# Weight decode in a top-k attention and ELU kernel: the sign word made on GpSimd and joined by VectorE

## The chip, the cores and the metric

The kernel runs on one core of a Trainium2 chip. The metric is device time in microseconds (us) of one execution; lower is better. Before the change three runs took 1666.97, 1667.17 and 1669.18 us, median 1667.17 us. The engines are named as in the profile: PE is TensorE (PEld its weight loads), DVE is VectorE, ACT is ScalarE, POOL is GpSimd, SP is SyncE, which here only issues DMAs.

## The reference

Attention over 8 batches, 8 heads, 576 positions and 64 dimensions per head, in which each query row keeps only its 32 largest scores, followed by a two-layer network with an ELU between its layers.

```python
def _attn_ref(q, k, v):
    B, H, S, D = q.shape            # 8, 8, 576, 64
    top_k = 32
    scores = (1.0 / np.sqrt(D)) * np.matmul(q, k.transpose(0, 1, 3, 2))
    kth = np.partition(scores, -top_k, axis=-1)[..., -top_k:-top_k + 1]
    scores = np.where(scores >= kth, scores, -1000000000.0)
    scores = scores - np.max(scores, axis=-1, keepdims=True)
    attn = np.exp(scores)
    attn = attn / (np.sum(attn, axis=-1, keepdims=True) + 1e-09)
    return np.matmul(attn, v).astype(np.float32)

def _moe_ref(x, w_in, w_out):       # x: 4608 x 512, w_in: 512 x 2048, w_out: 2048 x 512
    h = x @ w_in
    g = np.where(h > 0.0, h, np.exp(np.minimum(h, 0.0)) - 1.0)
    return (g @ w_out).astype(np.float32)
```

The two weight matrices arrive as 64-bit floats. The kernel gets each as pairs of 32-bit words (low word, high word) and has to make 32-bit floats of them on the chip before the network can use them. That decode is the part that the change touches.

## The kernel before, in words

**Attention.** The work is a list of steps; a step is one tile of 128 query rows for one pair of heads. For each step PE makes the scores (L299), ACT moves them to SBUF (L307), and DVE finds the 32 largest of each row: four MAX8 instructions with three MATCH_REPLACE8 between them, for each of the two heads (`select_row` in the first eight steps, lines 318 to 328; `select` afterwards, lines 341 to 353). Then `mask` makes two tiny operands on POOL (`neg` L366, `gap` L368) and runs Prelu and Exp on ACT (L369, L370); `normalise` runs five tiny POOL operations and two of 128x576 (L380 to L387); `turn` transposes on PE (L406) and copies on ACT (L407); `attend` multiplies by V on PE (L432) and ACT copies the result (L459).

**Network.** As soon as the attention output of a block of tokens is complete, its network pieces are queued: `hidden` (PE L504; ACT L514, L517, L519; DVE L476) and `project` (PE L529; ACT L538). `feed` lets pieces go by a plan of due steps, and only when enough weights are decoded (`decoded[0]`).

**Decode.** The two matrices are cut into 32 pieces of 128x512 numbers. `load_weight(i)` brings the raw piece, 512 KB of word pairs, into one of seven buffers named `raw` (L153, on SP's queue). In the raw tile the low and the high words alternate, so each of them is read with a step of two words. Before the change a piece then goes through:

- ACT L174: the low word, as an integer, to a float (Copy with scale and bias, so that the bits hold the low mantissa), in place
- ACT L175: the sign of the high word (Sign), written as one byte of fp8 into every eighth byte of the tile
- ACT L178: the magnitude of the high word (Abs with a scale), in place
- POOL L179: the magnitude held between a largest and a smallest value (min, max), in place
- DVE L186: the high word shifted left by three, in place
- POOL L187: the integer sum of the high and the low word, written to the final weight tile `w_in` or `w_out`

**Order.** `decode_piece(i)` issues the load of piece i+3, `convert_first(i)` (the first four operations) and `convert_last(i - 3)` (the last two). There are 35 such calls in a list. `hook()`, called by the selection after its later rounds, takes one from the list: four per step in the first eight steps (two for each head), then three in step 8. When the list is empty the raw buffers are closed and the network's larger tiles take their place. For the first two transposes and from step 8 on (`n == tight`) each engine's order is the program's; in between, in the first eight steps, a scheduler orders each engine's queue by readiness and program order at compile time. On the chip every engine then works its queue strictly in order.

Of the kernel before, what the change touches and what calls it, by code (L numbers as in the profile page):

```python
# [8 lines left out]
AF = mybir.ActivationFunctionType  # L9
ALU = mybir.AluOpType  # L10
FP32 = mybir.dt.float32
U32 = mybir.dt.uint32
I32 = mybir.dt.int32
FP8 = mybir.dt.float8e4
PSUM = bass.MemoryType.PSUM

TOP_K = 32
# [64 lines left out]
def kernel(  # L82
# [9 lines left out]
    nc = tc.nc  # L92
# [9 lines left out]
    NF = dff // P  # L102
# [3 lines left out]
    scale = 1.0 / float(D) ** 0.5  # L106
# [33 lines left out]
    raw = {}  # L140

    def weight(i):
        per = dff // WN
        if i < NC * per:
            f, c = divmod(i, NC)
            src = moe_w_in[c * P : (c + 1) * P, 2 * f * WN : 2 * (f + 1) * WN]
            return src, w_in[:, c, f * WN : (f + 1) * WN]
        f = i - NC * per
        return moe_w_out[f * P : (f + 1) * P, :], w_out[:, f, :]

    def load_weight(i):
        t = rawpool.tile([P, 2 * WN], U32, tag="raw", name="raw")
        nc.sync.dma_start(t[:], weight(i)[0])  # L153
        raw[i] = t

    def parts(t):
        words = t[:].rearrange("p (n w) -> p n w", w=2)
        signs = t[:].bitcast(FP8).rearrange("p (n w) -> p n w", w=8)
        return words[:, :, 0], words[:, :, 1], signs[:, :, 3]

    def convert_first(i):

        lo, hi, sign = parts(raw[i])
        ef, mf = hi.bitcast(FP32), lo.bitcast(FP32)
        nc.scalar.activation(mf, lo, AF.Copy, scale=2.0**-35, bias=2.0**17)  # L174
        nc.scalar.activation(  # L175
            sign, ef, AF.Sign, scale=2.0**64, bias=1.0, saturate=False
        )
        nc.scalar.activation(ef, ef, AF.Abs, scale=2.0**-62)  # L178
        nc.gpsimd.tensor_scalar(  # L179
            ef, ef, (2.0 - 2.0**-3 - 2.0**-23) * 2.0**-46, 2.0**-77, ALU.min, ALU.max  # L180
        )

    def convert_last(i):
        t, dst = raw.pop(i), weight(i)[1]
        lo, hi, sign = parts(t)
        nc.vector.tensor_single_scalar(hi, hi, 3, ALU.logical_shift_left)  # L186
        nc.gpsimd.tensor_tensor(  # L187
            dst.bitcast(I32), hi.bitcast(I32), lo.bitcast(I32), ALU.add
        )

    decode = []
    decoded = [0]
# [10 lines left out]
            late["x"] = ctx.enter_context(tc.tile_pool(name="xt", bufs=2))  # L203

    def decode_piece(i):
        if i < 2 * NF:
            if i + 3 < 2 * NF:
                load_weight(i + 3)
            convert_first(i)
        if i > 2:  # L210
            convert_last(i - 3)
            decoded[0] = i - 2

    loaded, kqT, vT = {}, {}, {}

# [200 lines left out]
    def attend(g):  # L416
# [28 lines left out]
        while tiles:  # L445
            blk, lo, parts = tiles[0].block, tiles[0].cols.start, 0
            while tiles and tiles[0].block is blk:
                parts += 1
                hi = tiles.pop(0).cols.stop
            finish(blk, parts, g.hp, slice(lo, hi), ps[:, c0 : c0 + hi - lo])  # L450
            c0 += hi - lo
# [106 lines left out]
    for b in range(B):  # L558
# [12 lines left out]
        for qt in range(J + 1):  # L571
# [8 lines left out]
            t = Tile(b, qt, rows, blk, slice(c0, c0 + n))  # L580
# [6 lines left out]
        for qts in order:  # L587
# [3 lines left out]
            for qt in qts:  # L591
                n = len(steps)
# [54 lines left out]
    for hp in range(1, NHP):  # L647
        load_v(0, hp)
    decode += [lambda i=i: decode_piece(i) for i in range(2 * NF + 3)]
    at(0, start_qk, 0, 2)  # L650
    at(1, start_qk, 0, 3)
# [93 lines left out]
```

## Time and profile before

| | value |
|---|---|
| median of three runs | 1667.17 us (1666.97 to 1669.18) |
| the profiled execution's own time | 1667.02 us |
| its span, first to last instruction | 1665.2 us |
| PE busy | 1592.8 us, 96% of the span |
| DVE busy | 1495.8 us, 90% |
| ACT busy | 1165.1 us, 70% |
| POOL busy | 630.5 us, 38% |
| mean granted TensorE clock | 0.977 |

Busy time is summed over the whole span, which hides that the stages differ. The kernel has three: an opening of some 150 us in which the 32 weight pieces are decoded beside the first nine steps; a long middle; and a tail of about 100 us without selection, in which PE finishes the last network blocks. The page cuts the span into 40 slices of 41.6 us; a digit is the busy share of a slice in tenths. A time stamp such as "at 57.39" counts in us from the span's start.

### The profile page before, as it was taken

The numbers are of one execution on the slowest core, as the hardware profiler recorded it, in microseconds if no ns is written. First come the engines' busy times: TensorE is split into PE (matmuls) and PEld (weight loads), VectorE is DVE, ScalarE is ACT, GpSimd is POOL, SyncE is SP. The second block draws the span as 40 slices with busy tenths as digits, with TensorE's granted clock in tenths as the row PEclk, the third lists the DMA queues.
The fourth block names the chain that finished last, engine by engine and source line by source line (L and its number), as shares of the span: only waits on it lengthen the run. The fifth ranks groups of instructions, "written<-read, shape, count | busy, mean of one in ns | idle before, by whom it ended". The sixth has DMA issues, their size and how long they took to land.

```text
span 1665.2 us, 25986 instructions
## 1 busy us (share of the span) xinstructions
PE 1592.8 (96%) x8528; PEld 1031.5 (62%) x8528; DVE 1495.8 (90%) x3044; ACT 1165.1 (70%) x2377; POOL 630.5 (38%) x1719
## 2 busy tenths in 40 slices
PE   5589999999999999999999999999999999999999
PEld 3366677657574767656566676755557575755565
DVE  5887999999999999999999999999999999998500
ACT  6998777668686777678667685868758585857521
POOL 3775444333334334333334333333333343332200
PEclk9578999999999999999999999999999999999999
DMA  7540120001100110001100111001200100000000
GB/s 211 171 144 7 23 50 29 7 15 44 48 1 8 43 42 22 1 28 37 42 14 1 50 29 35 1 14 43 50 13 1 28 15 29 7 7 7 7 13 13
DMA packets 101126, 56.21 MB, mean 34 GB/s; under 512 B 84096, under 2 KB 92288, under 8 KB 100992
## 3 DMA queue, kind: packets, MB, share of 16 engines
q1 hardware_dynamic: 99792, 54.26, 11.7%
q8 instruction: 68, 1.11, 0.3%
q14 instruction: 66, 0.54, 0.1%
q10 hardware_dynamic: 1200, 0.30, 0.1%
HBM read 45.09 MB, written 9.44 MB: 33 GB/s over the span
## 4 chain that ended last, share of the span: by engine, by line
PE 65%; DVE 21%; ACT 9%; POOL 3%; issue 2%; SPq 0%; DMA 0%; ACTq 0%; POOLq 0%; DVEq 0%
PE ops L529 24%; PE hps L504 20%; DVE wk L346 9%; DVE m L353 8%; PE avps L432 7%; PE scps L299 6%; PE eps L406 5%; DVE m L341 3%; ACT sc L370 2%; ACT sc L369 1%; DVE gT L476 1%; ACT raw L175 1%; PE qkps L269 1%; ACT et L407 1%; POOL w_in L187 1%
## 5 line engine op out<-in xcount | busy, mean ns | idle before, releaser
L353 DVE MAX8 m<-wk 128x8 f32<-128x576 f32 x816 | 577.0, 750 | 0.0
L504 PE MATMUL hps<-xT,w_in 128*128 128x256 f32 (+2 forms) x2432 | 548.1, 374 | 12.5 <-ACT xT L459 12.3
L529 PE MATMUL ops<-w_out,gT 128*128 128x512 f32 x1152 | 522.8, 598 | 0.0
L504 PEld LDWEIGHTS hps<-xT,w_in 128*128 128x128 f32 x2432 | 406.5, 193 | 109.2 <-issue 23.8
L346 DVE MATCH_REPLACE8 wk<-m,wk 128x576 f32<-128x576 f32 x544 | 400.8, 746 | 0.0
L529 PEld LDWEIGHTS ops<-w_out,gT 128*128 128x128 f32 x1152 | 208.7, 190 | 233.0 <-issue 219.5
L380 POOL TENSOR_SCALAR dene<-den 128x2 f32<-128x2 f32 x144 | 35.9, 249 | 771.2 <-ACT sc L370 770.6
L369 ACT ACTIVATE sc<-sc,neg 128x576 f32<-128x576 f32 x288 | 226.8, 788 | 89.2 <-POOL neg L366 89.0
L370 ACT ACTIVATE sc<-sc,gap 128x576 f32<-128x576 f32 x288 | 224.1, 778 | 25.7 <-ACT sc L369 0.7
L387 POOL TENSOR_SCALAR sc<-sc,rec 128x576 f32<-128x576 f32 x288 | 221.0, 778 | 14.9
L307 ACT ACTIVATE sc<-scps 128x576 f32<-128x576 f32 x288 | 174.0, 659 | 73.3 <-PE scps L299 73.3
L299 PE MATMUL scps<-kqT 64*128 64x288 f32 (+1 forms) x1280 | 201.8, 440 | 21.2 <-ACT kqT L275 7.9
L407 ACT COPY et<-eps 128x512 f32<-128x512 f32 x288 | 166.8, 579 | 55.2 <-PE eps L406 55.0
L346 DVE MATCH_REPLACE8 wk<-m,sc 128x576 f32<-128x576 f32 x272 | 200.4, 746 | 0.0
L432 PE MATMUL avps<-et,vT 128*64 128x256 f32 (+2 forms) x2080 | 193.3, 326 | 4.8 <-ACT et L407 4.6
L406 PEld LDWEIGHTS eps<-ident,sc 128*128 128x128 f32 x1152 | 143.6, 144 | 83.8 <-issue 46.2
L476 DVE SCALAR_TENSOR_TENSOR gT<-n,gT 128x512 f32<-128x512 f32 (+1 forms) x132 | 100.2, 759 | 102.0 <-ACT n L519 101.9
L341 DVE MAX8 m<-sc 128x8 f32<-128x576 f32 x272 | 191.8, 748 | 0.0
L406 PE MATMUL eps<-ident,sc 128*128 128x128 f32 x1152 | 175.7, 278 | 15.4 <-POOL sc L387 13.0
L432 PEld LDWEIGHTS avps<-et,vT 128*64 128x64 f32 x2080 | 122.6, 141 | 79.1 <-issue 22.8
L299 PEld LDWEIGHTS scps<-kqT 64*128 64x128 f32 (+1 forms) x1280 | 108.1, 181 | 91.9 <-issue 44.2
L514 ACT ACTIVATE n<-hps 128x512 f32<-128x512 f32 (+1 forms) x156 | 88.0, 564 | 71.4 <-PE hps L504 67.5
(47 smaller groups left out, 1170.2 us busy)
## 6 DMA issues: line engine op xcount, KB each, us to landing
kin<-in_k_dram SPq DMA_DIRECT2D x64, 128.0 KB, 2.8
raw<-in_moe_w_in_dram SPq DMA_DIRECT2D x16, 512.0 KB, 5.4
vT<-in_v_dram SPq DMA_DIRECT2D x64, 128.0 KB, 2.3
raw<-in_moe_w_out_dram SPq DMA_DIRECT2D x16, 512.0 KB, 3.9
out_dram<-osb SPq DMA_DIRECT2D x32, 256.0 KB, 2.3
qin<-in_q_dram SPq DMA_DIRECT2D x62, 128.0 KB, 2.8
kin<-in_k_dram SPq DMA_DIRECT2D x32, 32.0 KB, 2.4
vT<-in_v_dram SPq DMA_DIRECT2D x64, 16.0 KB, 2.2
```

Of the source, the lines that this page charges most:

```text
L299: nc.tensor.matmul(wide[i][rows, half, 0:HS], kq[part, q0 : q0 + u.t.ql], kq[part, k0 : k0 + HS], start=True, stop=True,)
L341: nc.vector.max(found[i], cur[i])
L346: nc.vector.match_replace(wk[i], found[i], cur[i], TAKEN)
L353: nc.vector.max(found[i], cur[i])
L369: nc.scalar.activation(sc, sc, AF.Prelu, bias=neg[:], alpha=STEEP)
L370: nc.scalar.activation(sc, sc, AF.Exp, bias=gap[:], accum_out=u.den[:, i : i + 1])
L387: nc.gpsimd.tensor_scalar(u.sc[:, i, :], u.sc[:, i, :], rec[:, i : i + 1], 1.0, ALU.mult, ALU.mult)
L406: nc.tensor.transpose(ps[:, c * P : (c + 1) * P], sc[:, c0 : c0 + P], ident[:])
L407: nc.scalar.copy(g.et[:, chunks, u.at, :], ps[:, 0 : n * P].rearrange("p (c q) -> p c q", c=n),)
L432: nc.tensor.matmul(ps[i * D : (i + 1) * D, cols], vt[:, 2 * J + i if c == J else i * J + c, :], w, start=(c == 0), stop=(c == J),)
L504: nc.tensor.matmul(blk.h[:, f % bank, :], w_in[:, i, f * P : (f + 1) * P], blk.xT[:, i, 0:n_tok], start=(i == 0), stop=(i == NC - 1),)
L529: nc.tensor.matmul(blk.o[:], blk.gT[f // NG][:, f % NG, s * P : (s + 1) * P], w_out[:, f, :], start=(f == 0), stop=(f == NF - 1),)
```

## The change

The sign is no longer made on ACT as a byte of fp8. The magnitude is written by ACT straight into the final weight tile. POOL holds it between its bounds there, and in a second, new operation multiplies the raw high word, taken as a float, by zero, which leaves a zero with the sign of the number. DVE's shift becomes a two-input operation that shifts the magnitude in the weight tile left by three and joins the sign word by exclusive or. POOL adds the low word in place. The four parts of a piece are now spread over four consecutive calls, instead of the first and the fourth.

```diff
     def convert_first(i):
-        lo, hi, sign = parts(raw[i])
-        ef, mf = hi.bitcast(FP32), lo.bitcast(FP32)
-        nc.scalar.activation(mf, lo, AF.Copy, scale=2.0**-35, bias=2.0**17)
-        nc.scalar.activation(
-            sign, ef, AF.Sign, scale=2.0**64, bias=1.0, saturate=False
-        )
-        nc.scalar.activation(ef, ef, AF.Abs, scale=2.0**-62)
-        nc.gpsimd.tensor_scalar(
-            ef, ef, (2.0 - 2.0**-3 - 2.0**-23) * 2.0**-46, 2.0**-77, ALU.min, ALU.max
+        lo, hi = parts(raw[i])
+        nc.scalar.activation(weight(i)[1], hi.bitcast(FP32), AF.Abs, scale=2.0**-66)
+        nc.scalar.activation(lo.bitcast(FP32), lo, AF.Copy, scale=2.0**-35, bias=2.0**17)
+
+    def convert_second(i):
+        w = weight(i)[1]
+        nc.gpsimd.tensor_scalar(
+            w, w, (2.0 - 2.0**-3 - 2.0**-23) * 2.0**-50, 2.0**-81, ALU.min, ALU.max
         )
+        ef = parts(raw[i])[1].bitcast(FP32)
+        nc.gpsimd.tensor_scalar(ef, ef, 0.0, 1.0, ALU.mult, ALU.mult)
+
+    def convert_third(i):
+        w = weight(i)[1].bitcast(U32)
+        nc.vector.scalar_tensor_tensor(
+            out=w, in0=w, scalar=3, in1=parts(raw[i])[1],
+            op0=ALU.logical_shift_left, op1=ALU.bitwise_xor,
+        )

     def convert_last(i):
-        t, dst = raw.pop(i), weight(i)[1]
-        lo, hi, sign = parts(t)
-        nc.vector.tensor_single_scalar(hi, hi, 3, ALU.logical_shift_left)
-        nc.gpsimd.tensor_tensor(
-            dst.bitcast(I32), hi.bitcast(I32), lo.bitcast(I32), ALU.add
-        )
+        w, t = weight(i)[1].bitcast(I32), raw.pop(i)
+        nc.gpsimd.tensor_tensor(w, w, parts(t)[0].bitcast(I32), ALU.add)
...
     def decode_piece(i):
-        if i < 2 * NF:
-            if i + 3 < 2 * NF:
-                load_weight(i + 3)
-            convert_first(i)
-        if i > 2:
-            convert_last(i - 3)
-            decoded[0] = i - 2
+        stages = (convert_first, convert_second, convert_third, convert_last)
+        if i + 3 < 2 * NF:
+            load_weight(i + 3)
+        for ago, stage in enumerate(stages):
+            if 0 <= i - ago < 2 * NF:
+                stage(i - ago)
+        decoded[0] = max(0, i - 2)
```

More of the change, by code (lines that the diff above doesn't have):

```diff
@@ L13 @@
 I32 = mybir.dt.int32
-FP8 = mybir.dt.float8e4
 PSUM = bass.MemoryType.PSUM
@@ L157, in parts @@
         words = t[:].rearrange("p (n w) -> p n w", w=2)
-        signs = t[:].bitcast(FP8).rearrange("p (n w) -> p n w", w=8)
-        return words[:, :, 0], words[:, :, 1], signs[:, :, 3]
+        return words[:, :, 0], words[:, :, 1]
     def convert_first(i):
-        lo, hi, sign = parts(raw[i])
-        ef, mf = hi.bitcast(FP32), lo.bitcast(FP32)
-        nc.scalar.activation(mf, lo, AF.Copy, scale=2.0**-35, bias=2.0**17)
-        nc.scalar.activation(
-            sign, ef, AF.Sign, scale=2.0**64, bias=1.0, saturate=False
-        )
-        nc.scalar.activation(ef, ef, AF.Abs, scale=2.0**-62)
-        nc.gpsimd.tensor_scalar(
-            ef, ef, (2.0 - 2.0**-3 - 2.0**-23) * 2.0**-46, 2.0**-77, ALU.min, ALU.max
+        lo, hi = parts(raw[i])
[5 more added lines that the diff above has]
+            w, w, (2.0 - 2.0**-3 - 2.0**-23) * 2.0**-50, 2.0**-81, ALU.min, ALU.max
+        )
+        ef = parts(raw[i])[1].bitcast(FP32)
[5 more added lines that the diff above has]
+            op0=ALU.logical_shift_left, op1=ALU.bitwise_xor,
         )
     def convert_last(i):
-        t, dst = raw.pop(i), weight(i)[1]
-        lo, hi, sign = parts(t)
-        nc.vector.tensor_single_scalar(hi, hi, 3, ALU.logical_shift_left)
-        nc.gpsimd.tensor_tensor(
-            dst.bitcast(I32), hi.bitcast(I32), lo.bitcast(I32), ALU.add
-        )
+        w, t = weight(i)[1].bitcast(I32), raw.pop(i)
+        nc.gpsimd.tensor_tensor(w, w, parts(t)[0].bitcast(I32), ALU.add)
     decode = []
```

## The prediction

> **What bounds the kernel now.** I read the page's 40 slices first, to see which engine is full in which stage.
>
> ```profile
> PE   5589999999999999999999999999999999999999
> DVE  5887999999999999999999999999999999998500
> ACT  6998777668686777678667685868758585857521
> POOL 3775444333334334333334333333333343332200
> ```
>
> The first four slices (to about 150 us) hold the decode, and there ACT is the full engine (9, 9) while DVE is not. Afterwards DVE is full, late in the run PE. So I cut the decode out: from the ACT start of piece 3 (36.7) to the last shift on DVE (148.1), 111.4 us with 29 of the 32 pieces. In these rows (busy time by stretch) come length, then PE, PEld, DVE, ACT and POOL, each with its count.
>
> ```profile
> 36.70:148.10 111.40, 78.07 (x393) 56.09 (x389) 83.16 (x172) 106.98 (x181) 75.19 (x125) 0.68 0.42 132
> 57.39:72.36 14.97, 10.78 (x43) 7.31 (x42) 12.75 (x26) 14.32 (x24) 11.18 (x20) 0.50 0.61 179
> 105.40:148.10 42.70, 35.20 (x191) 25.12 (x189) 27.92 (x58) 40.27 (x70) 25.27 (x42) 0.80 0.19 63
> 200.00:400.00 200.00, 192.40 (x1354) 138.32 (x1352) 200.00 (x413) 145.63 (x309) 77.82 (x223) 1.00 0.11 29
> 800.00:1000.00 200.00, 199.76 (x1045) 127.91 (x1044) 194.61 (x398) 139.98 (x289) 75.14 (x217) 1.00 0.10 26
> ```
>
> ACT is busy 106.98 of 111.4 us: it sets the pace. DVE idles 28.2 us and POOL 36.2. The last two rows say what a shift of the decode is worth: DVE has no idle time in 200 to 400 and PE 0.24 us in 800 to 1000, and the program's order is fixed there, so what the decode gains or loses comes out at the end one for one.
>
> The waits of the same stretch (total, times, longest) show the chain ACT to POOL to DVE:
>
> ```profile
> DVE raw L186 <- POOL raw L179: 22.3, 17, 4.0
> POOL raw L179 <- ACT raw L178: 20.0, 7, 5.8
> POOL neg L366 <- DVE m L328: 6.8, 5, 2.4
> ```
>
> And the groups of instructions there give the prices (count, total busy, mean ns, idle before):
>
> ```profile
> L175 ACT ACTIVATE raw<-raw 128x512 fp8e4<-128x512 f32 x29 | 37.1, 1424 | 0.0
> L179 POOL TENSOR_SCALAR raw<-raw 128x512 f32<-128x512 f32 x29 | 21.2, 730 | 21.8 <-ACT raw L178 20.0
> L187 POOL TENSOR_TENSOR w_out<-raw 128x512 int32<-128x512 int32 x15 | 16.4, 1106 | 1.3 <-DVE raw L186 0.8
> L187 POOL TENSOR_TENSOR w_in<-raw 128x512 int32<-128x512 int32 x13 | 14.1, 1094 | 2.4 <-DVE raw L186 2.0
> L186 DVE TENSOR_SCALAR raw<-raw 128x512 uint32<-128x512 uint32 x28 | 13.9, 501 | 22.3 <-POOL raw L179 22.3
> ```
>
> **What is taken away.** ACT loses Sign: 37.1 us of its 106.98, leaving 69.9 in 111.4. ACT is then no longer the pace, and POOL's 20.0 us of waiting for Abs goes. None of the 37 us counts by itself; what counts is who is late next. The Trainium skill ("ScalarE: Activation LUTs", "What ACT_TABLE_LOAD costs") gives every function 186 ns plus 0.833 ns per element, by which Sign would be an estimated 0.61 us and ACT would keep 89.2; the rows, with 1.42 for Sign beside 0.74 for Abs, disagree, and either way ACT is freed.
>
> **DVE.** The shift (mean 0.50) becomes a two-input operation. The nearest row is L476, the same instruction form on 128x512, median 0.69. 29 x 0.19 = 5.5 us, so DVE needs 88.7 of 111.4 us: hidden in its idle time, and uncovered only if the stretch fell below 89.
>
> **POOL.** It gains one operation per piece, the high word times zero: a one-input operation on 512 elements with the step that L179 reads now, median 0.658, plus some 0.05 to the next start: 0.71. Min/max and the sum keep their form and size, in the weight tile instead of the raw one; I cost that move at nothing. POOL's account of the stretch:
>
> - now: 75.2 busy, and hand-overs: in 57.39 to 72.36 it is idle 3.8 us, of which 2.9 are waits for DVE and 0.9 lies between 20 instructions, 0.045 each; 125 of them give 5.6, less what overlaps already, taken as 4.8. Sum 80.0.
> - less what the present shift costs it: beside a shift POOL's operations are longer. Their medians and maxima (min/median/max in ns):
>
> ```profile
> L179 POOL TENSOR_SCALAR raw<-raw x32: 638/658/923, 11.5 to 143.3; 128x512 f32<-128x512 f32 x32
> L186 DVE TENSOR_SCALAR raw<-raw x32: 401/429/1281, 12.2 to 148.1; 128x512 uint32<-128x512 uint32 x32
> L387 POOL TENSOR_SCALAR sc<-sc,rec x288: 739/750/1429, 33.3 to 1586.0; 128x576 f32<-128x576 f32 x144
> ```
>
>  Mean against undisturbed is 0.730 to 0.65 for 29 and 1.10 to 1.035 for 28: 4.1 us, 0.14 per shift on average, 0.24 where one hits (0.90 against 0.66).
> - plus 29 x 0.71 = 20.6.
>
> 80.0 - 4.1 + 20.6 = 96.5 us, before any hindrance by the new DVE operation and before any wait.
>
> **The hindrance.** The maxima above show two engines that stop each other: a shift of 0.43 took 1.28, an L387 of 0.75 took 1.43. For the new form, the trace shows L476 beside L387:
>
> ```profile
> 347.53 0.70 DVE L476 SCALAR_TENSOR_TENSOR gT<-n,gT 128x512 f32<-128x512 f32 x1
> 346.69 2.08 POOL L387 TENSOR_SCALAR sc<-sc,rec 128x576 f32<-128x576 f32 x2
> ```
>
> Two L387 alone take 1.48; here 2.08, so one STT (the two-input operation) of 0.70 cost POOL 0.60. The price per piece lies between 0.14 (the shift's average) and 0.61 (each one hits). The shifts hit about three in five times (0.14 of 0.24); with POOL near full more will, so I take three in four, 0.45: 29 x 0.45 = 13.1 us. The Trainium skill ("SBUF — State Buffer", "Who interferes with whom") speaks against this change: a DVE instruction with two SBUF inputs and a POOL instruction that reads SBUF exclude each other, for the whole instruction. By that rule the price would be an estimated 0.69 each, 20.0 us in all; the row shows a little less.
>
> **The waits.** The decode now passes ACT, POOL, DVE, POOL in four calls, with one call between neighbours; before, DVE's shift had three calls after the min/max. Behind a late multiply on POOL stands DVE's join, and behind that on DVE the next MAX8 and MATCH_REPLACE8, whose result POOL's own `neg` and `gap` wait for. Now POOL waits for DVE 6.8 us (`neg`) and 2.8 (L187): 9.6 us, 0.33 per piece. Its bounds are 0 (all data come a call earlier) and twice that. I keep 9.6.
>
> SP's raw loads (L153), and the k, q, v loads behind them on its queue, wait for POOL's last sum as they do now, seven buffers deep; a raw piece lands in 4.5 us (median) and is wanted three calls, some 11 us, later, so 6 us of POOL lateness stays hidden.
>
> **The sum.** 96.5 + 13.1 + 9.6 = 119.2 us against 111.4: 7.8 later. In the opening, ACT works two Signs (at 9.33 and 13.75, 1.2 from start to start) ahead of the first key copies and the first scores (L275 at 11.33, L307 at 15.67), which DVE's first MAX8 at 16.89 waits for. The second scores are ready on PE only at 14.73, so 1.5 us can come out, between 0 and 2.4. Net +6.3. The profiled execution took 1667.0 (span 1665.2 and 1.8 around it), which is also the median (1667.2): **1673.3 us**.
>
> **The rivals.**
>
> *Faster: POOL just carries it.* The change breaks even at (111.4 + 1.5 - 96.5) / 29 = 0.57 us of hindrance and waits per piece; I have 0.78. If POOL never waits, and hits stay at three in five (0.36 each), the stretch is 96.5 + 10.4 = 106.9, 4.5 shorter, and with the opening 1661.0; at 0.14 it would be 100.6 and 1654.7. For it: ACT's results are ready a call earlier, POOL has 36 us of idle now, and the last stretch (105.4 to 148.1, POOL 25.27 of 42.7) has room. Against it: in 57.39 to 72.36 POOL has 12.1 of 14.97 filled including hand-overs, and four multiplies add 2.8, so there 14.97 is passed by the four joins alone.
>
> *Much slower: a ring.* DVE waits for POOL's multiply, POOL for DVE's m. If the waits double (19.2) and every join hits (0.61, 17.7), the stretch is 133.4 and the time 1687.5. For it: the single call of slack, and that a `neg` wait of 2.4 stands in both of the steadiest steps (before 64.43 and 79.41). Against: POOL has two prepared operations per piece to work on meanwhile.
>
> *Nothing to see.* Within 0.2% (3.3 us, about what a measurement of this kernel can tell): hindrance and waits together at 0.57 per piece, give or take 3.3 / 29 = 0.11. My two terms need only be a little too large for it.
>
> **How the numbers follow.** My case (1670.5 to about 1681) has 0.48, the ring 0.13, the faster case 0.25, nothing 0.14. So slower 0.61, same 0.14, faster 0.25. For 8 in 10 the range goes down to 1659, inside the faster case, and up to 1686, nearly the ring's price.
>
> **What would show it.** Right: ACT's busy share from 36.7 to the end of decode falls to about 0.6 and POOL's rises above 0.85; the multiply at about 0.66; DVE's join with a minimum near 0.68 and a tail above 1.2; POOL's mean for its three decode operations above their medians; the largest DVE wait is the join on POOL's multiply; the last join at about 154. From there on DVE full as before, the same distance to the end. Wrong: a POOL that idles 20% or more while DVE waits (the ring), or a last join before 146 (the faster case). If the last join moves and the total doesn't follow, the one-for-one step is wrong.

## The result, and the profile after

The changed kernel takes 1683.57 us (median of four runs, 1682.71 to 1686.38) against 1668.18 (four runs, 1666.97 to 1669.41) before: a ratio of 1.0094 with a 95% interval of 1.0078 to 1.011, so 0.9% slower. The profiled executions, which carry every reading below, have spans of 1681.7 and 1665.2 us: 16.5 us. The prediction was 1673.3 in a range of 1659 to 1686.

The 40 slices of the changed kernel:

```profile
PE   5475999999999999999999999999999999999999
DVE  5788899999999999999999999999998999998600
ACT  5574877668776776768758685857758586757521
POOL 4987334333333334333334333333333333332200
```

The difference lies in the first four slices. ACT, full there before, falls to 5 and 7; POOL rises to 9, 8, 7; and PE falls to 4, 7, 5 where it had 5, 8, 9. The decode by stretches (length, then PE, PEld, DVE, ACT, POOL with counts, then the granted clock, the DMA share and GB/s):

```profile
36.70:148.10 111.40, 63.71 (x340) 47.10 (x339) 88.87 (x154) 71.28 (x139) 97.31 (x141) 0.66 0.41 129
36.70:153.70 117.00, 65.49 (x349) 48.87 (x348) 94.47 (x166) 71.91 (x141) 102.56 (x150) 0.65 0.39 123
140.00:150.00 10.00, 0.00 (x0) 0.00 (x0) 7.03 (x13) 5.89 (x12) 8.05 (x13) 0.50 0.00 1
150.00:160.00 10.00, 8.08 (x37) 5.78 (x38) 10.00 (x21) 5.07 (x11) 8.44 (x12) 0.50 0.01 2
200.00:400.00 200.00, 193.78 (x1374) 136.93 (x1373) 200.00 (x410) 144.42 (x306) 76.15 (x228) 1.00 0.11 29
```

In the 111.4 us of the prediction ACT now works 71.28 and POOL 97.31, and the stretch to the last join has become 117.0 us long. The third row is the surprise: from 140 to 150 PE executes nothing at all, and its granted clock is 0.50. Before, the same two stretches read

```profile
140.00:150.00 10.00, 10.00 (x37) 4.92 (x34) 10.00 (x22) 5.92 (x11) 4.68 (x6) 0.92 0.00 0
150.00:160.00 10.00, 10.00 (x53) 5.36 (x51) 10.00 (x21) 6.81 (x14) 5.49 (x16) 1.00 0.07 26
```

with PE and DVE both full. From 200 on (the last row of the changed kernel) DVE is full again: what was lost was lost before. Who waited, from 36.7 to the last join (total us, times, longest):

```profile
PE eps L407 <- POOL sc L388: 39.5, 6, 13.3
ACT et L408 <- PE eps L407: 20.8, 6, 7.1
ACT sc L370 <- POOL neg L367: 18.2, 8, 8.6
DVE w_in L183 <- POOL raw L178: 11.8, 7, 3.4
DVE w_out L183 <- POOL raw L178: 6.8, 4, 3.3
POOL w_out L174 <- ACT w_out L169: 5.8, 5, 1.5
POOL w_in L174 <- ACT w_in L169: 3.1, 1, 3.1
```

DVE's joins wait for the multiply (L178), 18.6 us together, as predicted. But the largest wait is PE's: its transposes (L407) wait 39.5 us for `normalise` (L388, which runs on POOL), once for 13.3 us. Before, the same wait was a third of that, with none above 3.4 us (waits from 36.7 to 148.1):

```profile
PE eps L406 <- POOL sc L387: 13.0, 5, 3.4
```

PE's timeline around the longest wait (start, us, line, what it waited for in brackets), changed kernel first, before second:

```profile
136.24 2.39 PE L433 MATMUL avps<-et,vT 128*64 128x128 f32 x18 [0.60 <-ACT et L408]
151.92 1.11 PE L407 MATMUL eps<-ident,sc 128*128 128x128 f32 x4 [13.29 <-POOL sc L388]
...
158.58 8.23 PE L530 MATMUL ops<-w_out,gT 128*128 128x512 f32 x16
```

```profile
138.78 2.40 PE L432 MATMUL avps<-et,vT 128*64 128x128 f32 x20
141.11 7.38 PE L529 MATMUL ops<-w_out,gT 128*128 128x512 f32 x16
```

PE's first `project` (L530; L529 before) moves from 141.11 to 158.58: 17.5 us, close to the whole loss. The transposes at 151.92 are those of step 6 (steps count from 0); before, they began at 132.21. POOL's timeline says what stood ahead of that `normalise`:

```profile
140.12 0.61 POOL L174 TENSOR_SCALAR w_out<-w_out 128x512 f32<-128x512 f32 x1 [1.49 <-ACT w_out L169]
140.81 0.64 POOL L178 TENSOR_SCALAR raw<-raw 128x512 f32<-128x512 f32 x1
142.70 0.61 POOL L174 TENSOR_SCALAR w_out<-w_out 128x512 f32<-128x512 f32 x1 [1.25 <-ACT w_out L169]
143.40 0.64 POOL L178 TENSOR_SCALAR raw<-raw 128x512 f32<-128x512 f32 x1
144.00 0.21 POOL L367 TENSOR_SCALAR neg<-m 128x1 f32<-128x1 f32 x1
...
145.76 1.28 POOL L190 TENSOR_TENSOR w_out<-w_out,raw 128x512 int32<-128x512 int32 x1
...
147.75 1.28 POOL L190 TENSOR_TENSOR w_out<-w_out,raw 128x512 int32<-128x512 int32 x1
148.99 0.72 POOL L383 TENSOR_TENSOR rec<-dene,power 128x2 f32<-128x2 f32 x1
...
151.11 1.48 POOL L388 TENSOR_SCALAR sc<-sc,rec 128x576 f32<-128x576 f32 x2
```

`neg`, a 0.21 us operation that ACT's exponentials need, stands in POOL's queue behind min/max and multiply of two pieces, which themselves wait for ACT (1.49 and 1.25 us). After the exponentials, the first operation of `normalise` (147.12) stands behind one sum of 1.28 us and its second behind another. Meanwhile PE is idle. Over the stretch ACT waits 20.8 us for PE's transposes, and up to the last magnitude (at 143.06) its next magnitudes stand in its queue behind such copies of PE's results; it also waits 18.2 us for `neg` directly. POOL, PE and ACT hold each other up in a circle.

The prices, from the groups of the same stretch (count, busy, mean ns, idle before):

```profile
L178 POOL TENSOR_SCALAR raw<-raw 128x512 f32<-128x512 f32 x29 | 19.7, 678 | 1.9
L190 POOL TENSOR_TENSOR w_out<-w_out,raw 128x512 int32<-128x512 int32 x13 | 18.1, 1397 | 0.2
L190 POOL TENSOR_TENSOR w_in<-w_in,raw 128x512 int32<-128x512 int32 x13 | 17.5, 1359 | 0.1
L183 DVE SCALAR_TENSOR_TENSOR w_out<-w_out,raw 128x512 uint32<-128x512 uint32 x16 | 14.4, 902 | 6.8 <-POOL raw L178 6.8
L183 DVE SCALAR_TENSOR_TENSOR w_in<-w_in,raw 128x512 uint32<-128x512 uint32 x13 | 14.3, 1100 | 11.9 <-POOL raw L178 11.8
```

and the records of three lines over the whole run (min/median/max in ns):

```profile
L190 POOL TENSOR_TENSOR w_in<-w_in,raw x16: 1277/1288/1760, 11.6 to 91.4; 128x512 int32<-128x512 int32 x16
...
L178 POOL TENSOR_SCALAR raw<-raw x32: 639/654/977, 10.1 to 145.1; 128x512 f32<-128x512 f32 x32
...
L183 DVE SCALAR_TENSOR_TENSOR w_in<-w_in,raw x16: 675/728/1776, 10.7 to 82.8; 128x512 uint32<-128x512 uint32 x16
```

The multiply has the forecast's price, and the join the forecast's minimum and tail. The sum (L190) does not: its minimum is 1.28 us, where before the change it was 1.03:

```profile
L187 POOL TENSOR_TENSOR w_in<-raw x16: 1032/1038/1301, 12.8 to 82.8; 128x512 int32<-128x512 int32 x16
```

### The profile page after: what moved, and what is told of

The parts are those of the page before. It is cut to its first block, busy times and chain, and to the rows that moved or that the text cites. A ratio compares the mean times of both kernels' runs of the same rounds, so it can differ in the third digit from the quotient of the medians.

```text
span 1681.7 us, 25946 instructions
## 1 busy us (share of the span) xinstructions
PE 1590.4 (95%) x8528; PEld 1030.0 (61%) x8528; DVE 1512.8 (90%) x3044; ACT 1131.2 (67%) x2345; POOL 659.4 (39%) x1751
## 3 DMA queue, kind: packets, MB, share of 16 engines
q1 hardware_dynamic: 99792, 54.26, 11.6%
## 4 chain that ended last, share of the span: by engine, by line
PE 71%; DVE 14%; ACT 6%; POOL 6%; issue 2%; SPq 1%; DMA 0%; ACTq 0%; POOLq 0%
PE ops L530 26%; PE hps L505 22%; PE avps L433 9%; PE scps L300 7%; DVE wk L347 6%; PE eps L407 5%; DVE m L354 5%; DVE m L342 2%; ACT sc L370 1%; ACT sc L371 1%; PE qkps L270 1%; DVE gT L477 1%; POOL raw L178 1%; ACT et L408 1%; POOL sc L388 1%
## 5 line engine op out<-in xcount | busy, mean ns | idle before, releaser
L530 PE MATMUL ops<-w_out,gT 128*128 128x512 f32 x1152 | 523.7, 600 | 0.0
L530 PEld LDWEIGHTS ops<-w_out,gT 128*128 128x128 f32 x1152 | 209.4, 191 | 233.2 <-issue 220.3
L388 POOL TENSOR_SCALAR sc<-sc,rec 128x576 f32<-128x576 f32 x288 | 220.8, 777 | 15.0 <-POOL rec L386 0.2
L407 PE MATMUL eps<-ident,sc 128*128 128x128 f32 x1152 | 176.0, 278 | 47.6 <-POOL sc L388 45.8
L407 PEld LDWEIGHTS eps<-ident,sc 128*128 128x128 f32 x1152 | 143.5, 144 | 116.2 <-POOL sc L388 48.4
```

Of the source, the lines that this page charges most:

```text
L388: nc.gpsimd.tensor_scalar(u.sc[:, i, :], u.sc[:, i, :], rec[:, i : i + 1], 1.0, ALU.mult, ALU.mult)
L407: nc.tensor.transpose(ps[:, c * P : (c + 1) * P], sc[:, c0 : c0 + P], ident[:])
L530: nc.tensor.matmul(blk.o[:], blk.gT[f // NG][:, f % NG, s * P : (s + 1) * P], w_out[:, f, :], start=(f == 0), stop=(f == NF - 1),)
```

## The experiments

Each kernel was timed against the kernel before on the same chip. "Span" is that of the profiled execution; in e9 and e12 that execution is 2 to 3 us quicker than the median. Two landmarks go with it: the start of PE's first `project` (before 141.1, changed 158.6) and the start of DVE's first MAX8 of step 9, the first step without decode (before 148.5, changed 157.4). Line numbers differ by kernel.

### e1: without the multiply

From the changed kernel:

```diff
-        ef = parts(raw[i])[1].bitcast(FP32)
-        nc.gpsimd.tensor_scalar(ef, ef, 0.0, 1.0, ALU.mult, ALU.mult)
```

> The changed kernel without the multiply by zero: the join takes the raw high word as it is, so the sign word is left out and the weights are not the reference's. Theory LOAD (POOL's added work alone sets the decode's pace and through its normalise the end): POOL loses 29 x 0.73 = 21 us of the stretch, the time falls by 15 to 21 us to 1663 to 1669, close to the kernel before. Theory STAGES (the four calls with one call between neighbours make DVE and POOL wait for each other, whatever their load): the waits stay, the time falls by less than 8 us, to 1676 or more.

Measured: 1666.64 us, ratio 0.9994 (0.9985 to 1.0003): all of the loss is gone. Its decode stretch, in the columns of before:

```profile
36.70:148.10 111.40, 74.39 (x388) 53.70 (x389) 94.56 (x180) 77.22 (x154) 91.55 (x131) 0.65 0.43 130
```

POOL falls from 97.31 to 91.55 us in the stretch although there is more of everything else in it, and PE rises from 63.71 to 74.39. Staging, the two-input join and the slower sum are all still there. So the multiply is worth 16.9 us (29 of them are 19.7 us busy in the groups above), and a theory by which the hand-overs of the four stages alone cost the time falls. The edit also takes away DVE's wait for the multiply; e8 and e9 below show that POOL's load is what counts.

### e4: the kernel before without Sign

```diff
-        nc.scalar.activation(
-            sign, ef, AF.Sign, scale=2.0**64, bias=1.0, saturate=False
-        )
```

> The kernel before, with ACT's Sign left out (the weights lose their sign): the relief of ACT without the price that the change pays for it. If ACT alone held the decode back, the next engines are DVE with 83 and POOL with 80 of 111 us: the decode ends 10 to 16 us earlier and so does the kernel, 1651 to 1657. If something else is right behind ACT (PE at half clock, the order of the queues), it gains less than 6 us, 1661 or more.

Measured: 1653.93 us, ratio 0.992 (0.9905 to 0.9935). PE's first `project` starts at 124.1:

```profile
124.14 7.13 PE L526 MATMUL ops<-w_out,gT 128*128 128x512 f32 x16
```

17.0 us earlier than before, and the span is 13.6 us shorter. This is the relief by itself: what taking Sign off ACT brings in this order of the program. All that the change adds is to be set against 13.5 us.

### e2: the sum with both inputs in the raw tile

```diff
-            out=w, in0=w, scalar=3, in1=parts(raw[i])[1],
+            out=parts(raw[i])[1], in0=w, scalar=3, in1=parts(raw[i])[1],
...
-        nc.gpsimd.tensor_tensor(w, w, parts(t)[0].bitcast(I32), ALU.add)
+        lo, hi = parts(t)
+        nc.gpsimd.tensor_tensor(w, hi.bitcast(I32), lo.bitcast(I32), ALU.add)
```

> The changed kernel with the join's result written back to the raw high word, so that POOL's sum reads two words of the raw tile and writes the weight tile, as before the change; all else the same, the result the reference's. It asks what the sum's 1.28 us (1.04 before) is worth. LOAD: the sum returns to 1.04, POOL loses 29 x 0.25 = 7 us, the time falls to 1675 to 1678. If the 1.28 is not the operands' place, the sum stays at 1.28 and so does the time. STAGES: the sum may return to 1.04 but the time stays within 2 us of 1683.6.

Measured: 1677.62 us, ratio 1.0062 (1.0047 to 1.0077), 6.0 us under the changed kernel. The records of the sum:

```profile
L191 POOL TENSOR_TENSOR w_in<-raw x16: 1028/1038/1486, 11.6 to 89.3; 128x512 int32<-128x512 int32 x16
```

The same sum, of the same size, is 0.25 us cheaper again when it reads both words from the raw tile. 26 sums of the stretch lie ahead of the last join: 26 x 0.25 = 6.5 us, and 6.0 of it shows in the time.

### e3: the two large operations of normalise on ACT in the first eight steps

```diff
         for i in range(2):
+            if on_act:
+                nc.scalar.activation(
+                    u.sc[:, i, :], u.sc[:, i, :], AF.Copy, scale=rec[:, i : i + 1]
+                )
+                continue
             nc.gpsimd.tensor_scalar(
...
-                    normalise(prev)
+                    normalise(prev, True)
```

> The changed kernel with the two 128x576 scalings of normalise done by ACT instead of POOL in the first eight steps; the result the reference's. PE stands idle for 13.3 us before 151.9 for exactly these. If the end is set by PE's wait for normalise behind POOL's decode work: PE's first project (158.6) comes 10 us or more earlier and the time falls to 1670 to 1674. If the end is set by DVE's last join (153.7) alone: that moves by POOL's relief too, but the total by less than 5 us, 1679 or more, because DVE then waits in step 9 for what PE still has to do.

Measured: 1676.8 us, ratio 1.0057 (1.0041 to 1.0074), 6.8 us better than the changed kernel. PE's timeline:

```profile
138.95 1.11 PE L412 MATMUL eps<-ident,sc 128*128 128x128 f32 x4 [3.49 <-ACT sc L389]
...
148.46 7.25 PE L535 MATMUL ops<-w_out,gT 128*128 128x512 f32 x16
```

The wait for `normalise` shrinks from 13.29 to 3.49 us here, and PE's first `project` comes 10.1 us earlier; but DVE's step 9 comes only 1.2 us earlier (156.3, which is 7.8 later than before), and then that is what the end follows. So the late `normalise` sets the end in the changed kernel, and behind it DVE allows no more than about 7 us of gain. Neither "PE alone" nor "DVE alone" is right.

### e7: the old staging in two calls

The four operations as in the change, but first and second in one call, third and fourth three calls later.

```diff
...
+            convert_first(i)
+            convert_second(i)
+        if i > 2:
+            convert_third(i - 3)
+            convert_last(i - 3)
```

> The changed kernel with the old calls: ACT's two, POOL's min/max and POOL's multiply in the first, DVE's join and POOL's sum in the fourth; the same instructions, the result the reference's. LOAD: POOL has the same work, the time stays within 4 us of 1683.6. STAGES (one call between neighbours is too little): three calls of slack for the join give back 8 us or more, 1676 or less.

Measured: 1679.17 us, ratio 1.0075 (1.006 to 1.009), 4.4 us better than the four calls, which lies between the two cases that I had written down. The staging is a minor part of the loss, and it is a loss, not a help.

### e8 and e9: a one-input shift in place of the join

e8 in the changed kernel; e9 the same in e1, without the multiply.

```diff
-        nc.vector.scalar_tensor_tensor(
-            out=w, in0=w, scalar=3, in1=parts(raw[i])[1],
-            op0=ALU.logical_shift_left, op1=ALU.bitwise_xor,
-        )
+        nc.vector.tensor_single_scalar(w, w, 3, ALU.logical_shift_left)
```

> The changed kernel with the join's second input left out: DVE shifts the weight tile in place (the weights lose their sign), POOL's multiply stays. POOL's operations show some 11 us of delay beside the joins in the changed kernel (0.39 per piece). If that hindrance comes from the two-input form: it falls to the shift's 0.14 per piece and the time by 5 to 9 us, to 1675 to 1679. If a shift hinders as much: within 3 us of 1683.6.

> e1_no_mult with the join's second input left out too: DVE shifts the weight tile in place, the weights have no sign. Against e1_no_mult (1666.6) only the form of DVE's operation differs; in both it waits for POOL's min/max alone, which e8_shift_only did not hold fixed: there the shift also stopped waiting for the multiply. If the two-input form hinders POOL more than a shift does: 4 to 8 us under e1, 1658 to 1662. If a shift hinders as much, and e8's 10 us came from the wait it drops: within 2 us of e1.

e8: 1673.54 us, ratio 1.0035 (1.0022 to 1.0048), 10 us better than the changed kernel and below what I had expected. But the records of its multiply show that two things changed:

```profile
L178 POOL TENSOR_SCALAR raw<-raw x32: 646/895/916, 10.1 to 148.7; 128x512 f32<-128x512 f32 x32
```

Its median has risen from 654 to 895 ns: a shift that need not wait for the multiply runs beside it, and nearly every one hits (28 of 32). e8 therefore does not isolate the join's two inputs. e9 does: in e1 and e9 alike nothing but min/max stands between ACT and DVE. e9 takes 1657.95 us, ratio 0.9939 (0.9926 to 0.9953), 8.7 us less than e1. Its shift:

```profile
L181 DVE TENSOR_SCALAR w_in<-w_in x16: 409/427/1008, 9.8 to 74.4; 128x512 uint32<-128x512 uint32 x16
```

Over 32 pieces that is 0.27 us per piece for the second input. What POOL's durations have above their undisturbed values (those of the shortest tenth of each operation), summed from 36.7 to the last join or shift, falls from 13.1 us (e1) to 7.2 (e9), so that 5.9 us of POOL's time go with the second input; how the other 2.8 come about wasn't tried.

e8 and e9 also settle what e1 left open. They differ in the multiply alone, and in e8 no engine waits for it; at 0.895 us each it still costs 15.6 us (1673.54 against 1657.95, with the kernel before at 1667.53 and 1667.57 beside them). So it is the multiply's load on POOL that costs the time, not DVE's wait for its result.

### The price list

In medians: before 1667.4 (with e1's runs), less Sign 1653.9 (e4), in the new form with a one-input shift and no sign word 1658.0 (e9), with the two-input join 1666.6 (e1), with the multiply 1683.6. In this order the relief is 13.5 us, and against it stand 4.1 for the new form, 8.7 for the second input of the join and 16.9 for the multiply. The dearer sum belongs to the 4.1 (alone it was worth 6.0 in e2 and, with POOL less loaded, 2.9 in e6 below); what else is in it wasn't separated.

### e5 and e6: a sign word of ACT's instead of POOL's

e5 puts a Copy on ACT in place of the multiply; e6 adds e2's sum.

```diff
+        ef = hi.bitcast(FP32)
+        nc.scalar.activation(ef, ef, AF.Copy, scale=0.0, bias=-0.0)
...
-        ef = parts(raw[i])[1].bitcast(FP32)
-        nc.gpsimd.tensor_scalar(ef, ef, 0.0, 1.0, ALU.mult, ALU.mult)
```

> The changed kernel with the sign word made by ACT instead of POOL: a Copy of the high word with scale 0.0 and bias -0.0, in place, in words of 32 bits, behind the two others in the first call. The result is the reference's if the zero keeps its sign. POOL is as in e1_no_mult; ACT has 32 x 0.67 = 21 us more, some 98 of 111. LOAD (POOL's work sets the pace): as e1_no_mult, 1664 to 1670. If ACT becomes the pace again: 1672 or more.

> e5_sign_act with e2_join_hi's change too (the join writes back to the raw word, the sum reads the raw tile and takes 1.04 again); the result as in e5. LOAD: POOL loses another 7 us, the time is 5 to 7 us under e5_sign_act, 1658 to 1663, faster than the kernel before. If ACT is the pace in e5 already: no more than 2 us under it.

e5: 1669.65 us, ratio 1.0015 (1.0006 to 1.0025). e6: 1666.78, ratio 0.9996 (0.9986 to 1.0005). The operation on ACT (records of e5):

```profile
L172 ACT ACTIVATE raw<-raw x32: 635/679/718, 9.5 to 142.3; 128x512 f32<-128x512 f32 x32
```

It is half of Sign's 1.42 us for the same number of elements, and the time still only comes back to about that of before (2.1 us above it), although with ACT at 91.81 of 111.4 us and POOL at 84.31 neither is full. The cheaper sum is worth 2.9 us here, where it was worth 6.0 in e2; my expectation of 5 to 7 was too high. My reading, which no run tests by itself, is that a POOL with room gives back less than one that sets the pace. These times show such an operation's cost only: the Copy did not carry the sign through, and the output is off by exactly as much as in e8 and e9, which leave the sign word out.

### e10 and e12: cheaper signs in the old form

e10 is the kernel before with the sign as a 16-bit float in the upper half of the low word, instead of one byte. e12 is the kernel before with Sign replaced by a byte operation on DVE, and Abs written to the weight tile.

```diff
-        signs = t[:].bitcast(FP8).rearrange("p (n w) -> p n w", w=8)
+        signs = t[:].bitcast(FP16).rearrange("p (n w) -> p n w", w=4)
...
```

```diff
+        nc.scalar.activation(w, ef, AF.Abs, scale=2.0**-62)
...
-        nc.scalar.activation(
-            sign, ef, AF.Sign, scale=2.0**64, bias=1.0, saturate=False
-        )
...
-        nc.vector.tensor_single_scalar(hi, hi, 3, ALU.logical_shift_left)
+        nc.vector.tensor_scalar(sign, top, 0x80, 0x38, ALU.bitwise_and, ALU.bitwise_or)
+        nc.vector.tensor_single_scalar(hi, dst.bitcast(U32), 3, ALU.logical_shift_left)
```

> The kernel before with one thing changed: Sign writes a 16-bit float into the upper half of the low word instead of an 8-bit one into its top byte (the constant moves the exponent by 8 more, so the magnitude's scale and its two bounds are halved); the result the reference's. If ACT's 1.42 us for Sign is the price of byte-wide writing: it falls to 0.7, ACT loses 21 us, nothing is added elsewhere, and the time falls by 8 to 12 us, near e4_no_sign, to 1655 to 1660. If it is the price of writing anything narrower than a word: no change, 1666 to 1669.

> A version made from what the runs showed: the kernel before without ACT's Sign, the sign byte made by DVE in one one-input operation (the top byte of the raw high word, and 0x80, or 0x38, written to the top byte of the low word), the magnitude written by ACT and bounded by POOL in the weight tile, and DVE's shift from there back to the raw high word, so that POOL has only min/max and a sum of two raw words. No multiply, no two-input operation on DVE; the result the reference's. DVE gets 29 x 0.43 to 0.6 = 12 to 17 us more where e4_no_sign leaves it 13.6 idle of 97.4. LOAD: between 1656 and 1663, faster than both kernels. If DVE, now the fullest, waits as often as in e4 (10.2 us for POOL): 1664 to 1668, no better than before.

e10: 1667.55 us, ratio 0.9999 (0.999 to 1.0008). Its Sign:

```profile
L175 ACT ACTIVATE raw<-raw x32: 1325/1410/1695, 9.8 to 139.7; 128x512 f16<-128x512 f32 x32
```

The price of Sign does not depend on one byte or two. e12: 1670.4 us (1666.2 to 1672.8), ratio 1.0013 (1.0004 to 1.0022), slower than both cases that I had written down. Its decode stretch, in an execution of 1667.6 us:

```profile
36.70:148.10 111.40, 75.99 (x387) 52.62 (x388) 104.89 (x203) 77.29 (x154) 81.65 (x126) 0.71 0.41 130
```

ACT and POOL both have room, but now DVE is the full engine, 104.89 of 111.4 us. The byte operation took 717/747/1548 ns (min, median, max), where I had expected 430 to 600. With e5 that makes three homes for the sign word (POOL, ACT, DVE), and as the only home none of them clearly beat the kernel before.

### e11: one piece in three the new way

The kernel before, with pieces 0, 3, 6 ... in the changed form (with e2's sum), and the others as before.

```diff
+    def new(i):
+        return i % 3 == 0
...
-            convert_first(i)
+            (new_first if new(i) else convert_first)(i)
```

> The kernel before with every third piece decoded the changed way (sign word on POOL, joined by DVE back into the raw word); the result the reference's. LOAD sees two lines that cross: ACT's, 1667.4 at no piece down to 1653.9 at all (e4), and POOL's, 1653.9 at no price up to 1677.6 at all (e2). At one third they give 1662.9 and 1661.8: the time is 1661 to 1665, faster than both kernels. If the changed way costs by its waits rather than its load, one third of it costs a third of its price on top: 1668 to 1672.

Measured: 1665.02 us, ratio 0.9982 (0.9973 to 0.9991), as expected (1661 to 1665) at its upper end.

```profile
36.70:148.10 111.40, 77.79 (x405) 55.67 (x402) 89.88 (x178) 96.90 (x173) 83.05 (x140) 0.68 0.43 133
```

ACT has 96.90 us (before 106.98), POOL 83.05 (75.19), DVE 89.88: no engine is full. Among the versions that keep the sign it is the one that beats both kernels, by 2.6 us over the one before; the interval excludes no change, though the size is just below the 0.2% that I had called measurable.

### What the end follows

The spans of the profiled executions, in us against that of the kernel before (1665.2), with the two landmarks against theirs:

| kernel | PE's first project | DVE's step 9 | span |
|---|---|---|---|
| after | +17.5 | +9.0 | +16.5 |
| e7 | +15.0 | +7.1 | +12.3 |
| e2 | +11.6 | +3.9 | +10.1 |
| e3 | +7.4 | +7.8 | +9.2 |
| e8 | +4.7 | +6.9 | +7.4 |
| e5 | +1.1 | +2.1 | +2.5 |
| e6 | -0.2 | +0.8 | +1.2 |
| e12 | +3.9 | -1.2 | +0.6 |
| e1 | +3.1 | -4.1 | +0.4 |
| e10 | -0.7 | -0.7 | -0.6 |
| e11 | -2.8 | -2.0 | -1.4 |
| e9 | -15.7 | -11.7 | -11.3 |
| e4 | -17.0 | -14.1 | -13.6 |

Where PE's landmark is the later one the span lies 1.0 to 3.3 us below it; where DVE's is, the span lies 0.4 to 1.4 above (in e10 the two move alike). The end follows the later of the two engines. That PE is the one in the changed kernel is also in the page's chain of work that ended last, where PE has 71% of the span, from 65% before, and DVE 14%, from 21%. Only e3 moves one landmark nearly by itself; the rest of the table is agreement, not proof. The mean granted clock fell as well, from 0.977 to 0.972, but the profiled execution of e1 has 0.972 too, with the span of before (1665.6): that alone does not make the loss.

## Why the prediction came out as it did

**ACT freed, POOL the pace: right.** To the end of the decode ACT's share is 71.91 / 117.0 = 0.61 (forecast about 0.6), POOL's 102.56 / 117.0 = 0.88 (above 0.85). e1, with e8 and e9, shows that POOL's load is what costs the time.

**The multiply: right.** Median 0.654 us, against 0.658.

**The hindrance: right in size, partly by luck.** POOL's operations take 12.8 us more than undisturbed (counted as in e9) up to the last join: 0.44 per piece, where the forecast was 0.45 and 13.1. But I had made the 0.45 of three joins in four at 0.60 each. In the trace 27 of the 29 joins meet a POOL instruction, and 28 POOL instructions are lengthened by 0.32 to 0.56 us each, which gives 11.9 of the 12.8. One join of the changed kernel, with POOL's rows around it:

```profile
47.62 1.28 POOL L190 TENSOR_TENSOR w_in<-w_in,raw 128x512 int32<-128x512 int32 x1
47.68 1.78 DVE L183 SCALAR_TENSOR_TENSOR w_in<-w_in,raw 128x512 uint32<-128x512 uint32 x1 [0.49 <-POOL raw L178]
48.98 0.94 POOL L174 TENSOR_SCALAR w_in<-w_in 128x512 f32<-128x512 f32 x1
```

The sum keeps its 1.28 us; the join beside it takes 1.78 instead of 0.68, and the min/max behind the sum 0.94 instead of 0.61. The Trainium skill's rule ("SBUF — State Buffer", "Who interferes with whom"), that a DVE instruction with two SBUF inputs and a POOL instruction that reads SBUF exclude each other for the whole instruction, agrees with these rows. A full 0.69 us lost for every piece, 20.0 us, was not seen.

**The waits: right in size, wrong in place.** I kept 9.6 us of POOL waiting for DVE. POOL waits 5.8 + 3.1 = 8.9 us, but for ACT's magnitudes, which stand in ACT's queue among copies of results that PE delivers late; none of its waits in that view names DVE. My ring ran between POOL and DVE; the one in the waits runs from POOL over PE and ACT, and e3, which takes the large operations of `normalise` off POOL, shortens PE's wait ahead of the first `project` from 13.29 to 3.49 us.

**"Min/max and the sum keep their form and size ... I cost that move at nothing": wrong.** The sum's median went from 1.04 to 1.29 us. I had a price for a sum of two words of the raw tile, and used it for one whose first input and output are the weight tile. The page of before has no such row, and I gave no bounds for it. 26 x 0.25 = 6.5 us of POOL; 6.0 at the end by e2.

**The stretch: 117.0 against 119.2, partly luck.** Against the uncounted 6.5 us stand two sums fewer ahead of the last join (26 where 28 were; 2 x 1.04 = 2.1 us), 29 x 0.045 = 1.3 us by which min/max is cheaper in the weight tile (median 0.613 against 0.658), and 1.8 us more that went with the old shift (5.9 us of hindrance over all POOL operations, where I took 4.1 from two lines). Waits and hindrance came out 1.0 below the forecast together, and some 2.5 us stay unexplained. So the last join came at 153.66, where I had said about 154.

**"What the decode gains or loses comes out at the end one for one": wrong, and this is the step that made the forecast too small.** The last join moved by 5.5 us and the end by 16.5. Two things went wrong. First, the last join is not the same place in DVE's queue: it now belongs to the last call but one, so that rounds of step 8 are still to come behind it. Before, step 9 began 0.3 us after the last shift, now 3.8 us after the last join, and DVE's step 9 is 9.0 later. Second, I argued from DVE that has no idle time afterwards, and did not ask when PE could begin its work. PE's transposes depend on POOL's `normalise`, and POOL's queue holds that behind the decode; a PE wait of 13.0 us for it stood in the waits of before, and I gave it no term. Two steps after that, in step 11 (from 178.7), DVE then waits for work of POOL and ACT that came late because PE was late (changed kernel, waits from 150 to 300):

```profile
ACT sc L308 <- PE scps L300: 11.8, 6, 7.4
...
DVE gT L477 <- ACT n L520: 4.7, 1, 4.7
...
DVE m L342 <- POOL gap L369: 1.9, 1, 1.9
```

9.0 + 4.7 + 1.9 = 15.6 us, and the next MAX8 after these (the 91st) starts at 186.87, 15.75 us later than before (171.12).

**The size.** Forecast +6.3, measured +16.5 between spans. Counted by price, with the sum at its old cost the kernel still has +10.1 (e2): of the missing 10 us about 6 are the sum and about 4 the step from the decode to the end. Counted by place, the last join came 5.5 us later (forecast 7.8) and 11.0 us more were lost behind it. The two counts overlap: a dearer sum also makes `normalise` later, and taking the large operations of `normalise` off POOL gives 6.8 us by itself.

**The opening.** First MAX8 at 15.89 instead of 16.89: 1.0 us, where I had 1.5.

**The rivals.** The faster case asked for POOL to carry it, with 0.57 us or less of hindrance and waits per piece. Measured were (12.8 + 8.9) / 29 = 0.75, and the sum came on top. The ring's doubled waits didn't come either, but its price (1687.5) was nearer to the result than my own case, because a ring I hadn't described was there. My own case reached to about 1681, and the result lies above that; it is inside the range only because I had stretched the range towards a ring of another kind. That part is luck.

## What to carry to other kernels

When a step is moved to an engine with idle time, list the tiny operations of the critical path that stand in that engine's queue (`neg`, `normalise`), and ask who idles while they stand behind the new work: here 0.65 us per piece, 21 us of POOL's time, became 17 us at the end, in part through PE's waits. Price an operation whose operands move to another tile as a new operation, with bounds, unless a row shows it with those operands. And where one engine is full and the next has room, moving part of the pieces (e11) can gain what moving all of them loses.

## What the runs showed of the hardware that I had not expected

- POOL's 32-bit integer sum over 128x512 takes 1.03 us with both inputs in one raw tile, each read with a step of two words, and 1.28 with the first input in the contiguous weight tile that it also writes (e2, and the changed kernel; the output is in that tile in both). Reading the contiguous tile was slower here. Whether it is the order of the words, the writing in place or inputs from two tiles, no run separates.
- ACT's Sign takes medians of 1.40 and 1.41 us on 512 elements written as one byte or two bytes with a step of eight bytes, while Copy and Abs of the same number of elements with 32-bit writes at that step take medians of 0.68 to 0.75 us (e5, e10). The Trainium skill ("ScalarE: Activation LUTs", "What ACT_TABLE_LOAD costs") gives one rate for every function, an estimated 0.61 us: near Copy and Abs, not Sign. Whether the narrow strided write or the function makes the difference stays open.
- ACT's Copy with scale 0.0 and bias -0.0, as these kernels write it, loses the sign of its input (e5, e6), where POOL's product of the high word with 0.0 keeps it.
- DVE's byte operation with a step of eight bytes takes 0.72 to 0.75 us for 512 elements (e12); the 32-bit shift of the same number takes 0.40 to 0.43.
- A one-input shift on DVE holds POOL up as well: the multiply rose from 0.654 to 0.895 us when nearly every shift met one (e8), 0.24 per hit.
- The granted clock of PE was 0.50 from 133.5 to 160.8 in the changed kernel. The fall came 5 us ahead of the 13.3 us without work, so that idle stretch did not set it off. The 16 matmuls of the first `project` began in it and took 8.23 us, against 7.38 before and 7.13 in e4; what that adds to the total no run separates.
